# Sliding-window attention into an RWKV channel mix: how the first q and k are loaded, which batches are transposed by the crossbar, and how the planner is set

## The chip, the cores and the metric

One core of a Trainium2 chip runs the whole kernel. The metric is the device time of one execution in microseconds (us). The kernel before takes 235.64 us (median of 14 runs, 234.65 to 236.24). The engines are TensorE (PE, matmul and transpose), ScalarE (ACT), VectorE (DVE), GpSimd (POOL, which here issues nearly all the loads), SyncE (SP, which issues stores and crossbar transposes) and 16 DMA engines.

## What is computed

q, k and v have 8 batches, 8 heads, 576 positions and a head dimension of 64, in fp32. Cut to what matters:

```python
scores = scale * q @ k.T                      # per batch and head
scores = where(0 <= i - j < 128, scores - slope[h] * abs(i - j), -1e9)
attn   = softmax(scores) @ v                  # causal window of 128
x      = attn, heads side by side             # [8, 576, 512]
x_prev = x shifted by one position
xk = mu_k * x + (1 - mu_k) * x_prev           # xr the same with mu_r
k  = relu(xk @ w_k)                           # 512 -> 1024
out = sigmoid(xr @ w_r) * ((k * k) @ w_v)     # 1024 -> 512
```

## The kernel before

**Stages.** Each of the eight batches is cut into four pairs of heads (g = 0 to 3). A pair goes through these steps: q and k are brought into a layout with the head dimension on the partitions; PE multiplies k by q (`scores`, L658), with the ALiBi bias added by a matmul (L645) in batch 0 and by a multiplication with a mask on DVE (L685) in the later batches; ACT takes the exponential (L672); PE multiplies by v (`attend`, L716), with a column of ones for the sum; DVE takes the reciprocal and scales (L722, L727); PE transposes the result (`out_t` L754 or `out_some` L771) and ACT copies it into `xt` (L628); DVE makes the difference and the two mixes `xk` and `xr` (`shift`, L814 and L821). `channel_mix` then does, for a stretch of 256, 384 or 512 positions, eight products with w_k (L907), each with a relu on ACT (L914) and a square on DVE (L880), and then for each 128 positions a product with w_r (L925, tanh on ACT, L932) and one with w_v in two halves (L941), joined on DVE (L946) and stored.

**How q and k come into that layout.** There are five ways. In batch 0 the work is done in two parts, positions 0 to 255 and the rest. In part 0 the first two pairs (g = 0, 1) are loaded as fp32 in runs of two positions (512 bytes), cast to bf16 by DVE (`CAST`) and transposed as bf16 (L1049); pairs 2 and 3, listed in `FT`, are loaded row by row (256 bytes) and transposed as fp32 by PE (L1046). Part 1 of batch 0 and the batches in `WIDE` are loaded with a cast on the way in long runs (`run_load`, L434) and transposed in 64 x 64 quarters (`qk_quad`, L1002), with two copies out of PSUM. Other batches are loaded row by row (`full_load`, L463) and transposed 128 x 128 (`qk_full`, L1154), with one copy. Batches in `XB` are loaded row by row and transposed by the DMA crossbar (`flip`). The last 64 positions (the tail) of q and k are loaded by `tail_load` (L453) and transposed on PE (L856), or by the crossbar for the batches in `XTT`.

**Order.** A planner simulates the kernel with its own costs and writes out each engine's instruction order; the engines then run in that order and wait on semaphores. Attention and channel mix compete by a rank: attention pair number 4b + g gets the key (4b + g - A) x SLOPE, with an A for each engine, and a piece of channel mix gets the sum of PE time of the channel mix ahead of it. A larger A puts attention further ahead. On PE, work in 64-row mode may be put off by `WAIT` so that it meets other work of that mode. Ninety matmuls of a dummy tile (L619, `warm`) have the lowest rank and fill PE where it has nothing else, early in the run.

**Loads.** POOL issues loads in one fixed order, after the first q (on SP's queue) and k (on ACT's queue). The string `LOADS` gives it for the first part: v and V are the halves of v of batch 0; 2 and 3 are part 1 of q and k, for heads 0 to 3 and 4 to 7; K and k are the halves of w_k; t is the tail of batch 0; a, b and c are q and k, tail, and v of batch 1; R is w_r; W and w are the halves of w_v. Batches 2 to 7 follow, each as a, b, c.

```python
    LOADS = 'v23KtVkabcRWw'
    A = {PE: 14.25, ACT: 4.00, DVE: 4.50, VIR: 0}
    WIDE = (1,)
    FT = (2, 3)
```

Of the kernel before, what the change touches and what calls it, by code (L numbers as in the profile page):

```python
# [179 lines left out]
def kernel(  # L180
# [12 lines left out]
    nc = tc.nc  # L193

    B, H, S, D = q.shape
    DM = H * D
    DF = moe_w_k.shape[1]
    G = H // 2
    NF = S // 128
# [7 lines left out]
    SM = 128 * NF  # L207
    RELU_SCALE = 0.5 ** 0.5

    PE, ACT, DVE, POOL, SPE, FAB, VIR = "PE", "ACT", "DVE", "POOL", "SP", "FAB", "VIR"  # L210
    NQ, NA, NX, NV, NC = 4, 4, 3, 2, 2
    XB = range(5, B)
    XO = range(6, B)
    X0 = 16
    NWARM = 90
    LOADS = 'v23KtVkabcRWw'
    XD = 6
    OTL = 1.5
    FIN = 384
    RATE = 284.0  # L220
    WIDE = (1,)
    PART_WIDE = True
    QUAD = 0.0565
    RUN = {2: 64 * 284 / 329.0, NF: 128 * 284 / 357.0}
    FLIP = 1.25
    NO = 5
    WAIT = 2.0
    QM = 0
    OM = 1

    def XU(b, g):
        return (DVE,)

    def SQ(order):
        return (DVE,)

    XT0 = (ACT,)
    QK0 = (ACT, DVE)
    CAST = (DVE,)
    FT = (2, 3)  # L240
    KQ = ACT
    VCUT = True
    XTT = range(6, B)
    MMASK = False
    VDEP = 1
    TCOST = 1.5
# [14 lines left out]
    ts_buf = many(2, [128, H, D], BF16, "ts")  # L261
    tt_buf = many(2, [128, G, 3, 64], BF16, "tt")
# [23 lines left out]
    ident = cst.tile([128, 128], BF16, name="ident")  # L286
# [16 lines left out]
    def one(h):  # L303
        return uno[h.idx if h.cls == "p1" else N1 + h.idx]

    def two(h):
        return duo[h.idx]

    plan = Plan(dict(qx=2, xb=2, p2=2, p1=N1, pt=4 - N1, qk=NQ, at=NA, xu=NX, vs=NV, cb=NC, ts=2, tt=2, xt=2, dl=2, dl0=4,
                     xk=2, rl=3, kk=3, rs=4, ot=NO),  # L310
                {}, WAIT)
# [5 lines left out]
    def act_t(n, sb=False):  # L317
        return (n + (112 if sb else 61)) / 1200.0

    def dve_t(n, fast=1):  # L320
        return (n / fast + 66) / 960.0

    AHEAD = 30.0
    A = {PE: 14.25, ACT: 4.00, DVE: 4.50, VIR: 0}
    NBIAS = 4
    XRL = 3.0
    MODE = 0
    EARLY = 0.0
    SLOPE = 4.5

    def rank(prio):

# [9 lines left out]
    def op(e, dur, deps, prio, emit, need=(), free=()):  # L342
        prio = rank(prio)
        return plan.add(e, dur, LAT.get(e, 0.2) if isinstance(e, str) else LAT[e[0]] if len(e) == 1 else 0.22,
                        deps, prio, emit, need, free)

    last = {}

    def virtual(key, holds):
        n = plan.add(VIR, 0.0001, 0.0001, [last.get(key)], (0,), None, holds)  # L350
        last[key] = n
        return n
# [11 lines left out]
    def dma(queue, kb, issue, emit, deps=(), need=(), free=(), lat=(1.0, 0.9)):  # L364
        n = plan.add(queue, issue, 0.0, list(deps) + [last.get(queue)],
                     (len(plan.nodes),), emit, need)
        last[queue] = n
        return fab(queue, kb / RATE, n, lat, free)
# [38 lines left out]
    n_ident = dve_op(0.11, emit_ident, [n_iota], (0, -1))  # L407
# [21 lines left out]
    def issue_t(nd):  # L429
        return 0.53 + 0.00034 * nd  # L430
# [16 lines left out]
    def tail_load(b):  # L447
        h = Hold("ts")
        g = virtual("ts", [h])
        ns = []  # L450
        for i in range(2):
            src = (q, k)[i][b, :, SM:S].rearrange("h p d -> p h d")
            ns.append(dma(POOL, 128 * TCOST, issue_t(512), lambda e, i=i, src=src: nc.gpsimd.dma_start(  # L453
                out=ts_buf[h.idx][64 * i:64 * i + 64], in_=src), [g]))
        return h, ns
# [4 lines left out]
    def full_load(b, i, h, g):  # L460
        src = (q, k)[i][b, :, 0:SM].rearrange(
            "h (r p) d -> p h r d" if b in XB else "h (p r) d -> p h r d", p=128)
        return [dma(POOL, 256, issue_t(1024), lambda e, r=r: nc.gpsimd.dma_start(  # L463
# [58 lines left out]
    th, tl, n_w, src1 = {}, {}, {}, {}  # L522
# [31 lines left out]
    cw, ch, cl, xbh, xbl, tth, ttl, ttg = {}, {}, {}, {}, {}, {}, {}, {}  # L554
# [10 lines left out]
    def batch_load(b, what):  # L565
# [7 lines left out]
        elif what == "b":  # L573
            th[b], tl[b] = tail_load(b)
            if b in XB:
                xbh[b] = Hold("qx")
# [20 lines left out]
    for (c0, n) in DSEG:  # L597
        n_copy[c0] = dve_op(dve_t(n, 4), lambda e, c0=c0, n=n: nc.vector.tensor_copy(
            out=dist[:, c0:c0 + n], in_=dist[:, 0:n]), [n_dist], (0, 1))
    n_sid = [dve_op(0.1, lambda e, h=h: nc.vector.tensor_scalar(  # L600
        out=sid[:, h], in0=ident, scalar1=-(2.0 ** (-(h + 1))) / scale, scalar2=None,
# [6 lines left out]
    def emit_mu(e):  # L608
# [5 lines left out]
        out=mu_sb.rearrange("p i o -> p (i o)"), in_=one(h_mu)[:, 0:2 * NPO]), (), [h_mu])  # L614
# [12 lines left out]
    def copy_any(e, out, in_):  # L627
        (nc.scalar.copy if e == ACT else nc.vector.tensor_copy)(out=out, in_=in_)  # L628
# [213 lines left out]
            res.append(fab(SPE, 1.0 * rows / 128, n, (1.0, 0.9), [hx]))  # L842
        return res

    def tails(b, prio):
        htt = Hold("tt")
        hs = th[b]
        if b in XTT:
            plan.follow(last["tt"], ttg[b])
            last["tt"] = ttg[b]  # L850
            return tth[b], ttl[b]
        hp = Hold("p1")

        def emit(e):
            for g in range(G):
                nc.tensor.transpose(  # L856
                    one(hp).bitcast(BF16)[:, 128 * g:128 * g + 128],
                    ts_buf[hs.idx][:, 2 * g:2 * g + 2].rearrange("p h d -> p (h d)"), ident)

        def emit_c(e):  # L860
            copy_any(e, tt_buf[htt.idx][:, :, 0:2].rearrange("p g t c -> p g (t c)"),
                     one(hp).bitcast(BF16)[:, 0:128 * G].rearrange("p (g w) -> p g w", g=G))

        t = op(PE, 0.0565 * G, list(tl[b]) + [n_ident], prio + (0,), emit, [hp], [hs])
        g = virtual("tt", [htt])
        c = [op(DVE, dve_t(512), [t, g], prio + (0,), emit_c, (), [hp])]
        return htt, c


# [2 lines left out]

    n_hw = 39 + sum(4 if g in FT else 2 for g in range(3)) + 8 * len(XB) + len(XTT) + NJ * len(XO)
    n_split = -n_hw % 8
# [119 lines left out]
    def qk_quad(b, g, nr, buf, deps, prio, c0, hq, take, free):  # L994

        hp = [Hold("p1"), Hold("p1")]

        def emit(e):
            for n in range(2 * nr):
                for hl, r in ((0, 0), (1, 1), (1, 0), (0, 1)):  # L1000
                    rows = slice(64 * r, 64 * r + 64)
                    nc.tensor.transpose(  # L1002
                        one(hp[r]).bitcast(BF16)[64 * hl:64 * hl + 64, 64 * n:64 * n + 64],
                        buf()[rows, n // nr, 2 * g + hl, n % nr], ident[rows, rows])

        t = op(PE, QUAD * 2 * nr, list(deps) + [n_ident], prio + (3,), emit,
               hp + ([hq] if take else []), free)
        t.rows, t.lazy = (64, 64), True
        w = 64 * nr
        ys = [op(QK0 if b == 0 else ACT, {ACT: act_t(2 * w), DVE: dve_t(2 * w)}, [t], prio + (3,),  # L1010
                 lambda e, r=r: copy_any(
            e, qk_buf[hq.idx][:, :, c0 + w * r:c0 + w * r + w].rearrange("p t (c r) -> p t c r", r=nr),
            one(hp[r]).bitcast(BF16)[:, 0:2 * w].rearrange("p (t r c) -> p t c r", t=2, r=nr)),
                 (), [hp[r]]) for r in range(2)]
        return hq, ys
# [6 lines left out]
    for part in range(2):  # L1022
        if part == 1:
            htt, n_tt = tails(0, (0, 0, 1, 0))
        for g in range(G):
            prio = (0, 0, part, g)
# [12 lines left out]
            hp = Hold("p1") if part == 0 else None  # L1039
# [13 lines left out]
            if part:  # L1053
                ys = qk_quad(0, g, 2, lambda: part_buf, cs, prio, 256, hq0[g], False, [])[1]
            else:
                cold = 1.8 if part == 0 and g < 2 else 1.0
                t = op(PE, (0.115 if f32 else 0.0565) * 4 * cold, cs + [n_ident], prio + (3,), emit_t,
                       [hp] + ([hq0[g]] if part == 0 else []))
                ys = [op(QK0, {ACT: act_t(512), DVE: dve_t(512)}, [t], prio + (3,),
                       lambda e, part=part, g=g, hp=hp, f32=f32: copy_any(  # L1060
                    e, qk_buf[hq0[g].idx][:, :, 0:256],
                    one(hp).rearrange("p (t c) -> p t c", t=2)) if f32 else copy_any(
                    e, qk_buf[hq0[g].idx][:, :, 256 * part:256 * part + 256].rearrange(
                        "p t (c r) -> p t c r", r=2),
                    one(hp).bitcast(BF16)[:, 0:512].rearrange("p (t r c) -> p t c r", t=2, r=2)),
                    (), [hp])]
            ha = Hold("at")
            es = []
            for j, (pieces, m0) in enumerate(PART[part]):
# [8 lines left out]
            r, hx = attend(0, g, t0, t1, ha, es + vl[0][0:2] + (vl[0][2:] + blank if part else []),  # L1078
                           prio)
            a, c = out_t(0, g, t0, t1, hx, [r], prio, xh[0], xth[0], late if part == 0 else None)  # L1080
# [31 lines left out]
    for j, (c0, n) in enumerate(MSEG):  # L1112
        n_mcopy.append(op(DVE, dve_t(8 * n, 4), ms + n_mcopy, (2, j),
                          lambda e, c0=c0, n=n: nc.vector.tensor_copy(
            out=mask[:, 0:H, c0:c0 + n], in_=mask[:, 0:H, 0:n])))
# [48 lines left out]
    for b in range(1, B):  # L1164
# [6 lines left out]
        htt, n_tt = tails(b, (0, b, 0, 0))  # L1171
        for g in range(G):
            prio = (0, b, 0, g)
            ha = Hold("at")
            if b in XB:
                hq, y = xbh[b], xbl[b]
# [13 lines left out]
            r, hx = attend(b, g, 0, NJ, ha, [m0, m1] + vl[b] + rs[0:1], prio)  # L1190
# [60 lines left out]
```

The softmax here doesn't subtract the row's maximum and nothing guards it: scores larger than these inputs give would overflow.

## Time and profile before

| | us |
|---|---|
| median of 14 runs | 235.64 (234.65 to 236.24) |
| the profiled execution | 235.28 |
| its span, first to last instruction | 233.2 |
| PE busy | 225.6 |
| DVE busy | 189.2 |
| ACT busy | 160.7 |
| POOL busy | 97.7 |

Busy time is what an engine's instructions cover in the span. A PE instruction is shown with its latency, so that two neighbours overlap, and what one costs is the distance from its start to the next one's; gaps shorter than that latency, and the dummy matmuls, count as busy. In a row of the order of time, the first number is the start, the second the length of the group, and "xN" how many instructions it holds. The granted clock is 0.999.

### The profile page before, as it was taken

Reading aid. Unit: us, or ns where it says so; the run is one execution under the profiler, and the core shown is the slowest. Engines: PE = TensorE matmul, PEld = TensorE weight load, DVE = VectorE, ACT = ScalarE, POOL = GpSimd, SP = SyncE. Lnnn points to the kernel's source line nnn. Section 1 sums busy time; section 2 is a strip of 40 time slices with the busy share of each in tenths; the row PEclk is TensorE's granted clock in tenths of the full one; section 3 lists DMA queues with packets and bytes.
Section 4 is the critical chain, followed back from the end, with each engine's and each line's share of the span. In section 5 each row is a group of like instructions: output and inputs, shape, how many; then the busy total and the mean of one; then the engine's idle time right before and its main releaser. Section 6 shows DMA issues by size and latency. Waiting matters only on the chain.

```text
span 233.2 us, 6268 instructions
## 1 busy us (share of the span) xinstructions
PE 225.6 (97%) x2487; PEld 135.7 (58%) x2487; DVE 189.2 (81%) x427; ACT 160.7 (69%) x292; POOL 97.7 (42%) x124
## 2 busy tenths in 40 slices
PE   8899989999999999999999999999999999999994
PEld 6466765456565765555555755454655844455462
DVE  7577978987897989989989979985869996974242
ACT  3569999759998986984984975947594726326251
POOL 8967683898882893068608845200000000000000
PEclk9999999999999999999999999999999999999999
DMA  7999999999999999779999999993242124121122
GB/s 167 178 170 196 163 173 182 155 201 199 155 138 174 105 143 203 112 93 175 205 150 135 172 176 170 172 155 122 70 92 93 45 48 146 46 90 48 64 71 90
DMA packets 131100, 31.73 MB, mean 136 GB/s; under 512 B 120056, under 2 KB 127232, under 8 KB 131072
## 3 DMA queue, kind: packets, MB, share of 16 engines
q0 software_dynamic: 102736, 16.26, 101.6%
q1 hardware_dynamic: 26592, 14.50, 27.1%
q10 hardware_dynamic: 1744, 0.59, 1.0%
q8 instruction: 19, 0.31, 0.6%
q14 instruction: 9, 0.07, 0.1%
HBM read 33.56 MB, written 9.44 MB: 184 GB/s over the span
## 4 chain that ended last, share of the span: by engine, by line
PE 87%; ACT 5%; DMA 2%; DVE 2%; issue 2%; SPq 1%; DVEq 0%; ACTq 0%
PE uno L941 27%; PE uno L907 26%; PE uno L925 14%; PE duo L716 6%; PE duo L658 6%; DMA qx<-in_q_dram 2%; PE uno L771 2%; PE uno L1154 2%; ACT at L672 2%; ACT mask L1088 1%; ACT qk L628 1%; PE uno L856 1%; ACT xt L628 1%; ACT rl L914 1%; PE uno L619 1%
## 5 line engine op out<-in xcount | busy, mean ns | idle before, releaser
L941 PE MATMUL uno<-wv_sb,kk 128*128 128x512 bf16 (+2 forms) x296 | 71.8, 374 | 0.0
L907 PE MATMUL uno<-xk,wk_sb 128*128 128x256 bf16 (+2 forms) x416 | 69.5, 314 | 0.6 <-ACT rl L914 0.4
L672 ACT ACTIVATE at<-duo 128x1024 bf16<-128x1024 f32 (+2 forms) x68 | 65.8, 1005 | 5.4 <-PE duo L658 5.4
L914 ACT ACTIVATE rl<-uno 128x256 bf16<-128x256 f32 (+2 forms) x104 | 47.4, 494 | 20.2 <-PE uno L907 19.0
L907 PEld LDWEIGHTS <-wk_sb 128*128 128x128 bf16 x416 | 38.7, 98 | 22.1 <-issue 0.9
L685 DVE TENSOR_TENSOR at<-at,mask 128x1024 bf16<-128x1024 bf16 x56 | 37.8, 681 | 8.1 <-ACT at L672 7.8
L438 POOL DMA_DIRECT2D vs<-in_v_dram x32 | 28.3, 898 | 34.1 <-PE duo L716 31.5
L941 PEld LDWEIGHTS <-kk 128*128 128x128 bf16 x296 | 26.4, 98 | 26.2
L880 DVE TENSOR_TENSOR kk<-rl 128x256 bf16<-128x256 bf16 (+2 forms) x104 | 33.1, 336 | 9.3 <-ACT rl L914 8.0
L932 ACT ACTIVATE rs<-uno 128x512 bf16<-128x512 f32 x36 | 22.2, 616 | 26.1 <-PE uno L925 23.1
L925 PE MATMUL uno<-wr_sb,xr 128*128 128x512 bf16 x144 | 37.0, 379 | 0.5 <-ACT rl L914 0.5
L946 DVE SCALAR_TENSOR_TENSOR ot<-rs,uno 128x512 f32<-128x512 bf16 (+2 forms) x37 | 24.7, 669 | 12.1 <-PE uno L941 9.7
L716 PEld LDWEIGHTS <-at 128*128 128x128 bf16 x576 | 21.8, 98 | 6.0 <-issue 0.9
L821 DVE SCALAR_TENSOR_TENSOR xk<-dl,mu_sb,xt 128x576 bf16<-128x576 bf16 (+1 forms) x32 | 24.8, 781 | 0.4
L821 DVE SCALAR_TENSOR_TENSOR xr<-dl,mu_sb,xt 128x576 bf16<-128x576 bf16 (+1 forms) x32 | 24.5, 771 | 0.0
L463 POOL DMA_DIRECT2D cb<-in_k_dram x24 | 21.3, 908 | 7.2 <-DMA wv_sb<-in_moe_w_v_dram 3.3
L628 ACT COPY xt<-uno 128x256 bf16<-128x256 bf16 (+1 forms) x48 | 17.1, 406 | 9.0 <-PE uno L771 8.8
L925 PEld LDWEIGHTS <-xr 128*128 128x128 bf16 x144 | 13.5, 98 | 14.6 <-issue 0.7
L463 POOL DMA_DIRECT2D cb<-in_q_dram x24 | 21.3, 921 | 1.2 <-DMA vs<-in_v_dram 1.0
L628 ACT COPY qk<-uno 128x1024 bf16<-128x1024 bf16 (+2 forms) x26 | 18.9, 779 | 2.5 <-PE uno L1002 1.1
L716 PE MATMUL duo<-vs,at 128*128 128x65 bf16 x448 | 19.1, 193 | 0.0
L814 DVE TENSOR_TENSOR dl<-xt 128x576 bf16<-128x576 bf16 (+1 forms) x32 | 13.8, 435 | 4.2 <-ACT xt L628 4.2
(78 smaller groups left out, 206.1 us busy)
## 6 DMA issues: line engine op xcount, KB each, us to landing
out_dram<-ot SPq DMA_DIRECT2D x30, 256.0 KB, 5.1
vs<-in_v_dram POOLq DMA_DIRECT2D x32, 128.0 KB, 7.0
cb<-in_q_dram POOLq DMA_DIRECT2D x24, 128.0 KB, 7.2
cb<-in_k_dram POOLq DMA_DIRECT2D x24, 128.0 KB, 7.2
out_dram<-ot SPq DMA_DIRECT2D x10, 128.0 KB, 1.8
wk_sb<-in_moe_w_k_dram POOLq DMA_DIRECT2D x2, 512.0 KB, 8.9
wv_sb<-in_moe_w_v_dram POOLq DMA_DIRECT2D x2, 512.0 KB, 10.2
qx<-in_k_dram ACTq DMA_DIRECT2D x4, 128.0 KB, 4.6
```

Source lines behind the costliest of these rows:

```text
L438: return dma(POOL, 256, issue_t(1024), lambda e: nc.gpsimd.dma_start(out=vs_buf[h.idx][:, j, :, 0:D], in_=v[b, :, 128 * j:128 * j + 128].r ...
L463: return [dma(POOL, 256, issue_t(1024), lambda e, r=r: nc.gpsimd.dma_start(out=cb_buf[h.idx][:, i, r], in_=src[:, :, r]), [g]) for r in ra ...
L628: (nc.scalar.copy if e == ACT else nc.vector.tensor_copy)(out=out, in_=in_)
L672: lambda e, ah=ah, w=w, hp=hp: nc.scalar.activation(out=ah(), in_=two(hp)[:, :, 0:w], func=AF.Exp, scale=float(scale)), (), [hp])
L685: nc.vector.tensor_tensor(out=a, in0=a, in1=m, op=ALU.mult)
L716: nc.tensor.matmul(a[:, hl, t - t0], lhsT=at[:, lo:lo + 128], rhs=vs[:, u, 2 * g + hl, :] if u < NF else tvb[:, 2 * g + hl], start=(u == u ...
L821: lambda e: nc.vector.scalar_tensor_tensor(out=buf[hk.idx][:, g, e0 + c0:e0 + c1], in0=dls(), scalar=mu[:, g:g + 1], in1=xc(1), op0=ALU.mu ...
L880: nc.vector.tensor_tensor(out=out, in0=in_, in1=in_, op=ALU.mult)
L907: nc.tensor.matmul(one(hp)[:, 0:n], lhsT=wk_sb[:, po, 128 * fo:128 * fo + 128], rhs=xk_buf[hx.idx][:, po, c0:c1], start=(po == 0), stop=(p ...
L914: a = op(ACT, act_t(n), [s], pr, lambda e, hp=hp, hr=hr: nc.scalar.activation(out=rl_buf[hr.idx][:, 0:n], in_=one(hp)[:, 0:n], func=AF.Rel ...
L925: nc.tensor.matmul(one(hp), lhsT=xr_buf[hx.idx][:, po, 128 * c:128 * c + 128], rhs=wr_sb[:, po], start=(po == 0), stop=(po == NPO - 1))
L941: nc.tensor.matmul(one(hv)[:, a:b], lhsT=kk_buf[hk.idx][:, fo, o:o + 128], rhs=wv_sb[:, fo, a:b], start=(fo == 0), stop=(fo == NFO - 1))
```

## The change

All four pairs of batch 0's part 0 are loaded in 512-byte runs and cast by DVE (`FT` is empty). Batch 2 joins batch 1 in the long-run load and the quarter transposes. Batches 3 and 4 go from `qk_full` to `qk_some` (two pairs in one go, 64-row transposes, `QM` = 2), and so does batch 5, which leaves the crossbar. The result of attention goes from `out_some` to `out_t` (128-row transposes, one copy, `OM` = 0). Tails of batches 4 and 5 go to the crossbar. The tail of batch 0 is loaded in runs of four positions and transposed by 16 small matmuls. Copies of q and k of batches 1 and 2 may go to DVE as well as ACT, and squares of the first three stretches to ACT as well as DVE. The first half of w_k is loaded ahead of part 1 of q and k, and w_r ahead of v of batch 1. The planner's leads, slope, waits and costs change.

```diff
-    XB = range(5, B)
+    XB = range(6, B)
...
-    LOADS = 'v23KtVkabcRWw'
-    XD = 6
+    LOADS = 'vK23tVkabRcWw'
+    XD = 4
...
-    WIDE = (1,)
+    WIDE = (1, 2)
...
-    QUAD = 0.0565
-    RUN = {2: 64 * 284 / 329.0, NF: 128 * 284 / 357.0}
+    QK1 = (ACT, DVE)
+    TW = (0,)
+    QUAD = 0.040
+    RUN = {2: 64 * 284 / 345.0, NF: 128 * 284 / 390.0}
...
-    WAIT = 2.0
-    QM = 0
-    OM = 1
+    WAIT = 1.0
+    QM = 2
+    OM = 0
...
-        return (DVE,)
+        return (DVE, ACT) if order < 3 else (DVE,)
...
-    FT = (2, 3)
+    FT = ()
...
-    XTT = range(6, B)
+    XTT = range(4, B)
...
-    A = {PE: 14.25, ACT: 4.00, DVE: 4.50, VIR: 0}
+    A = {PE: 7.75, ACT: 4.50, DVE: 4.00, VIR: 0}
...
-    XRL = 3.0
+    XRL = 4.0
...
-    SLOPE = 4.5
+    SLOPE = 4.7
...
+        if b in TW:
+            for i in range(2):
+                ns.append(dma(POOL, 104, issue_t(128), lambda e, i=i: nc.gpsimd.dma_start(
+                    out=ts_buf[h.idx].rearrange("p h d -> p (h d)")[:, 256 * i:256 * i + 256],
+                    in_=(q, k)[i][b, :, SM:S].rearrange("h (c r) d -> h c (r d)", r=4)), [g]))
+            return h, ns
...
+    def tails_full(b, prio, htt, hs):
...
+        if b not in TW:
+            return tails_full(b, prio, htt, hs)
         hp = Hold("p1")
         def emit(e):
+            for n in range(8):
+                for hl in range(2):
+                    nc.tensor.matmul(
+                        one(hp)[64 * hl:64 * hl + 64, 64 * n:64 * n + 64],
+                        lhsT=ts_buf[hs.idx][:, n],
+                        rhs=ident.rearrange("p (g t c) -> p t g c", g=G, t=2)[:, hl],
+                        start=True, stop=True)
...
+        c = [op(DVE, dve_t(256), [t, g], prio + (0,), lambda e, i=i: copy_any(
+            e, tt_buf[htt.idx][:, :, i].rearrange("p g (c r) -> p g c r", r=4),
+            one(hp)[:, 256 * i:256 * i + 256].rearrange("p (r g c) -> p g c r", r=4, g=G)),
+                (), [hp]) for i in range(2)]
...
-        ys = [op(QK0 if b == 0 else ACT, {ACT: act_t(2 * w), DVE: dve_t(2 * w)}, [t], prio + (3,),
+        ys = [op(QK0 if b == 0 else QK1, {ACT: act_t(2 * w), DVE: dve_t(2 * w)}, [t], prio + (3,),
```

More of the change, by code (lines that the diff above doesn't have):

```diff
@@ L843, in out_flip @@
         return res
[L845 to L851, printed above, removed]
+    def tails_full(b, prio, htt, hs):
         hp = Hold("p1")
@@ L866, in tails, with emit @@
         c = [op(DVE, dve_t(512), [t, g], prio + (0,), emit_c, (), [hp])]
+        return htt, c
+    def tails(b, prio):
+        htt = Hold("tt")
+        hs = th[b]
+        if b in XTT:
+            plan.follow(last["tt"], ttg[b])
+            last["tt"] = ttg[b]
+            return tth[b], ttl[b]
+        if b not in TW:
+            return tails_full(b, prio, htt, hs)
+        hp = Hold("p1")
+        def emit(e):
+            for n in range(8):
[5 more added lines that the diff above has]
+                        start=True, stop=True)
+        t = op(PE, 0.03 * 16, list(tl[b]) + [n_ident], prio + (0,), emit, [hp], [hs])
+        g = virtual("tt", [htt])
+        c = [op(DVE, dve_t(256), [t, g], prio + (0,), lambda e, i=i: copy_any(
+            e, tt_buf[htt.idx][:, :, i].rearrange("p g (c r) -> p g c r", r=4),
+            one(hp)[:, 256 * i:256 * i + 256].rearrange("p (r g c) -> p g c r", r=4, g=G)),
+                (), [hp]) for i in range(2)]
         return htt, c
```

## The prediction

> **What bounds the kernel now.** I read the page's busy totals first, then busy time by stage, then the longest waits, then the order of time in the first 40 us.
>
> ```profile
> PE 225.6 (97%) x2487; PEld 135.7 (58%) x2487; DVE 189.2 (81%) x427; ACT 160.7 (69%) x292; POOL 97.7 (42%) x124
> 20.00:30.00 10.00, 9.38 (x222) 7.44 (x221) 8.65 (x28) 9.71 (x28) 7.09 (x10) 1.00 2.03 168
> 30.00:40.00 10.00, 9.05 (x146) 6.56 (x146) 7.64 (x21) 9.67 (x20) 5.89 (x7) 1.00 1.55 187
> 40.00:230.00 190.00, 189.72 (x1868) 109.48 (x1866) 157.87 (x317) 129.60 (x226) 69.32 (x83) 1.00 1.25 127
> ```
>
> The columns of the last three lines are PE, its weight loads, DVE, ACT, POOL. From 40 us to 230 us PE is busy for 189.72 of 190 us: whatever PE work is added or removed there moves the end one for one, and nothing else does. From 20 to 40 us ACT is the full engine (9.71 and 9.67 of 10), with DVE at 8.65 and 7.64. Ahead of 20 us (PE 7.81 and 9.65) PE's busy time is partly the dummy matmuls. So there are two sums: PE work, and how soon the first 40 us get real work into PE.
>
> ```profile
> 7.78 1.07 PE L1046 MATMUL uno<-id,qx 128*128 128x128 f32 x7 [0.85 <-DMA qx<-in_q_dram]
> 8.68 0.39 PE L619 MATMUL uno<-warm 128*128 128x128 bf16 x4
> 9.26 0.61 PE L716 MATMUL uno<-vs,at 128*128 128x65 bf16 x12 [0.20 <-DVE qk L628]
> 13.52 0.84 PE L619 MATMUL uno<-warm 128*128 128x128 bf16 x12
> 15.95 0.83 PE L619 MATMUL uno<-warm 128*128 128x128 bf16 x12
> 18.96 0.61 PE L907 MATMUL uno<-xk,wk_sb 128*128 128x256 bf16 x4
> ```
>
> The fp32 pairs arrive at 7.7 us, and PE waits for them. Of the 90 dummies 57 come after 8.6 us; at 56 ns each that is 3.2 us of filler. The first channel mix starts at 18.96 us. By distances between starts, PE spends some 10 us between 4 and 40 us on filler and waits.
>
> [...]
>
> ```profile
> 50.00 1.04 PE L941 MATMUL uno<-wv_sb,kk 128*128 128x512 bf16 x4
> 50.97 0.32 PE L771 MATMUL uno<-ident,xu 64*128 64x64 bf16 x10
> 51.22 0.62 PE L1154 MATMUL uno<-ident,cb 128*128 128x128 bf16 x8
> 51.68 1.03 PE L941 MATMUL uno<-wv_sb,kk 128*128 128x512 bf16 x4
> 52.54 0.39 PE L856 MATMUL uno<-ident,ts 128*128 128x128 bf16 x4
> 52.76 1.50 PE L1154 MATMUL uno<-ident,cb 128*128 128x128 bf16 x24
> ```
>
> Four L941 take 0.86 us between neighbours of the same mode (51.68 to 52.54) but 0.97 before the 64-row L771: 0.10 into the mode, about 0.12 out of it. [...] in the DMA view of 2 to 8 us the queues move 283 to 340 GB/s while the 512-byte runs of pairs 0 and 1 arrive, and 184 to 276 when the 256-byte rows follow. [...]
>
> **The change, part by part: PE after 40 us.**
> - Results of attention, batches 1 to 5, 20 pairs. Ten 64-row transposes take 0.15 us beside scores (which are in that mode anyway), and about 0.14 + 0.22 = 0.36 alone. In the order of time 12 stand beside scores and 8 alone: 12 x 0.16 + 8 x 0.36 = 4.8 us. The five 128-row transposes at 56 ns (eight L1154 take 0.46) are 0.28: 5.6 us. **+0.8.**
> - q and k of batches 3 and 4. Before: 8 x 0.45 = 3.6 us. After: four groups of 32 64-row transposes. The row of L771 gives 14.4 ns each, so 0.46, and 0.02 to 0.22 of mode change: 1.9 to 2.7. **-1.3.**
> - Batch 5 leaves the crossbar: two such groups. **+1.15** (0.96 to 1.35).
> - Batch 2 in quarters: 32 quarter transposes take 0.34 to 0.40 us by the L1002 rows, plus mode change 0.02 to 0.22, against 0.45. Four pairs: -0.4 to +0.7. **0** taken.
> - Tails of batches 4 and 5: two L856 groups at 0.22 (52.54 to 52.76). **-0.45.**
>
> The sum is +0.2 us; ends -1.2 and +1.8. ACT, DVE and SP carry the rest under PE after 40 us: one copy of 576 columns in place of 428 + 383 ns, two copies of 620 ns in place of one of 1045 per pair, eight crossbar transposes fewer and two more. ACT has 60 us free there, DVE 32. If that cover went, DVE would be the first to be late.
>
> **The first 40 us.**
> - Load of pairs 2 and 3. 2048 packets of 256 B become 1024 of 512 B. At 230 and 320 GB/s the 0.52 MB take 2.3 and 1.6 us: **0.7 earlier**, so 7.0 us. Then two DVE casts per pair (0.42 each) replace none: g = 2 is cast at 7.9, transposed by 8.2 and copied by 8.9, where before its two products started at 10.13 (behind the attend at 9.26 that waited on DVE's 0.69 us fp32 copy). I take **0.8 us** earlier for both pairs. DVE's memsets end at 7.15 in the kernel before, so the casts find it free; were they late, the gain would be 0. PE's eight fp32 transposes (138 ns apart) become eight of 56: 0.6 us in a stretch with slack.
> - w_k ahead of part 1. The POOL issue moves it past four loads (0.76 us each), and they move past it: one issue (0.78) and 512 KB of bf16 at the 175 GB/s of that stretch, 2.9 us. Part 1's first quarter transposes were at 11.10, so the data that came by about 10.7 now comes at 13 to 13.6 (0.7 is given back by the shorter first loads). The four groups of that transpose were at 11.10, 13.27, 15.58 and 17.46, so three of four have room; what is queued behind the first on PE is attend and the output transposes of part 0, which go ahead in the new order. In exchange channel mix can start as soon as xk of part 0 is there. I cost the exchange at 0, with -1 to +2 us as its ends.
> - Tail of batch 0: 1024 packets of 128 B become 256 of 512 B; at 150 and 195 GB/s that is 0.87 against 0.67 us. Sixteen matmuls in place of four transposes and two DVE copies in place of one stand where the dummies stood: 0.
> - q and k of batch 1 come about 0.9 us earlier (0.7 + 0.2). Their first transpose waited until 25.47.
> - w_r ahead of v of batch 1: w_r lands some 6 us earlier, and L925 (first at 37.57) can fill PE. v is pushed back by 512 KB at 197 GB/s, 2.7 us: from 33.3 to 35.1 with the 0.9 above. The first attend of batch 1 was at 36.37, which leaves 1.2 us. w_v does not move by order, only by the 0.9: L941 could not start before it in either kernel.
> - ACT in 20 to 40 us: eight copies of q and k at 0.62 us (5.0 us); if DVE takes half, ACT is freed of 2.5 us and DVE pays 4 x 0.69 = 2.8 of its 3.7 free. One copy for two in `out_t` gives 4 x 0.16. ACT's stage shortens by up to 3 us; what is late next is DVE, then v and w_v. I take half: **1.5 us**.
>
> Sum: -0.8 - 1.5 + 0.2 = **-2.1 us**. From the profiled execution's 235.28 (span 233.2, 2.1 around it) that is 233.2, and against the median, 0.36 higher, **233.5 us**. Runs of this kernel scatter by 0.3%, so I call within 0.2% (0.5 us) the same.
>
> **The rivals.**
> 1. *The shorter lead makes it slower.* On PE attention's lead falls from A = 14.25 to 7.75. The channel mix is 62 + 31 + 62 = 156 us of PE, 4.9 per pair, 19.5 per batch. The last pair of batch b ranks at 18b - 51 before and 18.8b - 22 after, against its own mix at 19.5b: some 51 us of cover become 22. A pair's path from scores to xk is some 8 to 10 us in the trace when nothing stands in front, and ACT's and DVE's own leads are short. DVE is at 9.8 of 10 in some stretches (40 to 50, 90 to 100 us). If a batch boundary catches PE without mix work, each of the six boundaries costs about 1 us: minus 2 becomes plus 4, 239; with half of them, 237. For it: the cover is more than halved. Against: 22 us is still twice the path. It decides once queueing adds more than 12 us to the path.
> 2. *The early gain is hidden.* PE cannot have its w_v work before w_v lands (about 38 us) and v of batch 1 comes later; what ACT and DVE save is waited away. Then only the PE sum (+0.2) and 0.3 to 0.8 of start remain: 235.6 + 0.2 - 0.5 = 235.3. This includes that the casts don't bring pairs 2 and 3 forward.
> 3. *The start gains more.* The exchange of w_k gives its whole 1 us, ACT's stage its 3 us, and grouping with scores brings the PE sum to -0.2: 235.6 - 0.8 - 1 - 3 - 0.2 = 230.6.
>
> **How the numbers follow.** Forecast (232 to 235.1): 0.47. Rival 3: 0.10. Rival 2: 0.14. Rival 1, with its milder forms: 0.29. Faster by over 0.2%: 0.57; within: 0.13; slower: 0.30. The range reaches down to rival 3's end and up through the milder half of rival 1: 230.6 to 238.0. The forecast's own range is 232 to 235.1.
>
> **What would show it.** Right: first scores of pairs 2 and 3 near 9 us instead of 10.1; channel mix starting near 16 to 17 us instead of 18.96 and fewer dummies after 8 us; ACT below 9.5 of 10 in 20 to 40 us, with q and k copies on DVE; PE still over 99% busy from 40 us. Wrong: PE idle in the middle, ended by DVE's xk, xr or squares (rival 1); PE's start of full occupation still at 40 us (rival 2); or more mode changes than I counted for the 64-row groups.

## The result, and the profile after

The changed kernel takes 237.93 us (median of 10 runs, 237.28 to 238.38) against 235.50 for the kernel before beside it (48 runs). The ratio is 1.01, with a 95% interval of 1.0083 to 1.0118: slower by 1%, where I had forecast 0.9% faster. The profiled execution has a span of 235.8 us against 233.2.

The page's busy totals, and busy time by stage (PE, its weight loads, DVE, ACT, POOL), of the kernel after:

```profile
PE 225.8 (96%) x2615; PEld 138.0 (59%) x2615; DVE 190.4 (81%) x420; ACT 166.3 (71%) x302; POOL 93.6 (40%) x120
20.00:30.00 10.00, 9.69 (x211) 7.54 (x210) 8.12 (x24) 10.00 (x30) 6.21 (x9) 1.00 1.62 188
30.00:40.00 10.00, 9.90 (x170) 7.30 (x160) 9.17 (x18) 10.00 (x23) 5.85 (x8) 1.00 1.76 182
40.00:230.00 190.00, 186.65 (x1964) 109.55 (x1964) 156.04 (x311) 133.98 (x230) 66.19 (x79) 1.00 1.19 123
```

From 20 to 40 us PE idles only 0.4 us, where it idled 1.6 before. ACT, which I expected to be relieved, is at 10.00 of 10. And from 40 to 230 us, where PE was busy for 189.72, it is busy for 186.65: 3.1 us of new idle time. The first 20 us, of the kernel before (two rows) and of the kernel after (two rows):

```profile
0.00:10.00 10.00, 7.81 (x79) 5.87 (x79) 6.63 (x39) 4.55 (x6) 8.49 (x17) 1.00 1.23 169
10.00:20.00 10.00, 9.65 (x180) 6.33 (x179) 7.99 (x25) 7.14 (x16) 6.92 (x10) 1.00 1.80 180
0.00:10.00 10.00, 7.75 (x87) 5.63 (x88) 7.45 (x42) 4.86 (x7) 8.68 (x17) 1.00 1.06 172
10.00:20.00 10.00, 9.22 (x188) 6.43 (x185) 8.16 (x26) 6.87 (x16) 6.65 (x10) 1.00 1.83 172
```

These rows say where the time went. Up to 40 us PE is busy for 35.9 us before and for 36.6 us after, with the same 90 dummies in both and none of them later: the start gained 0.7 us. PE's busy total grew by 0.2 us (225.6 to 225.8). After 40 us PE idles 3.1 us more. 0.2 - 0.7 + 3.1 is 2.6 us, the difference of the two spans. So the whole loss stands after 40 us. The waits of PE there in the kernel after, in us in total, times, longest (the kernel before has one, of 0.2):

```profile
PE uno L937 <- DVE xk L829: 1.8, 1, 1.8
PE duo L724 <- ACT at L680: 0.7, 1, 0.7
PE uno L955 <- ACT qk L636: 0.6, 1, 0.6
PE uno L937 <- ACT rl L944: 0.2, 1, 0.2
```

The first three are the w_k product of the last batch (211 us), an attend (78 us) and a w_r product (67 us). ACT's order of time around the w_r product shows three copies of q and k in a row behind two exponentials; PE waits for one of these copies:

```profile
63.41 1.96 ACT L680 ACTIVATE at<-duo 128x1024 bf16<-128x1024 f32 x2
65.23 1.60 ACT L636 COPY qk<-uno 128x512 bf16<-128x512 bf16 x3
66.65 2.03 ACT L680 ACTIVATE at<-duo 128x1024 bf16<-128x1024 f32 x2
```

The wait at 211 us is for DVE. DVE's order puts joins of the channel mix (`ot`) between the pieces of the last batch's shift, and DVE sits idle for 2.46 us ahead of the first of them:

```profile
202.11 0.69 DVE L976 SCALAR_TENSOR_TENSOR ot<-rs,uno 128x512 f32<-128x512 bf16 x1 [2.46 <-PE uno L971]
209.77 0.68 DVE L976 SCALAR_TENSOR_TENSOR ot<-rs,uno 128x512 f32<-128x512 bf16 x1
210.37 0.81 DVE L829 SCALAR_TENSOR_TENSOR xk<-dl,mu_sb,xt 128x576 bf16<-128x576 bf16 x1
```

SP, too, issues its last five crossbar transposes into `xt` later, from 193.95 us on and not from 189.04.

What ACT had taken on, by the groups of ACT in the kernel after with their shapes:

```profile
L636 ACT COPY qk<-uno 128x512 bf16<-128x512 bf16 x37 | 21.6, 631 | 3.4 <-PE uno L1079 2.5 <-PE uno L1032 0.9
L908 ACT ACTIVATE kk<-rl 128x256 bf16<-128x256 bf16 x12 | 5.1, 487 | 0.0
L908 ACT ACTIVATE kk<-rl 128x384 bf16<-128x384 bf16 x3 | 1.5, 563 | 0.0
```

L908 is the square, which was on DVE alone. Fifteen of them, 6.6 us, now stand on ACT. A square of 256 columns takes 487 ns there; on DVE it took 283 in the kernel before. Of the sixteen 512-column copies of q and k of batches 1 and 2 only six went to DVE.

### The profile page after: what moved, and what is told of

Its sections match the earlier page's. It is cut to its first block, busy times and chain, and to the rows that moved or that the text cites. A ratio compares the mean times of both kernels' runs of the same rounds, so it can differ in the third digit from the quotient of the medians.

```text
span 235.8 us, 6507 instructions
## 1 busy us (share of the span) xinstructions
PE 225.8 (96%) x2615; PEld 138.0 (59%) x2615; DVE 190.4 (81%) x420; ACT 166.3 (71%) x302; POOL 93.6 (40%) x120
## 4 chain that ended last, share of the span: by engine, by line
PE 82%; ACT 5%; DVE 4%; DMA 4%; POOL 3%; issue 1%; DVEq 0%; POOLq 0%; ACTq 0%
PE uno L971 25%; PE uno L937 25%; PE uno L955 13%; PE duo L724 6%; PE duo L666 6%; DMA ts<-in_k_dram 4%; PE uno L762 2%; POOL qx L436 1%; ACT qk L636 1%; ACT rl L944 1%; DVE ot L976 1%; PE duo L653 1%; DVE xk L829 1%; ACT at L680 1%; POOL vs L440 1%
## 5 line engine op out<-in xcount | busy, mean ns | idle before, releaser
L680 ACT ACTIVATE at<-duo 128x1024 bf16<-128x1024 f32 (+2 forms) x68 | 64.4, 996 | 7.4 <-PE duo L666 7.3
L944 ACT ACTIVATE rl<-uno 128x256 bf16<-128x256 f32 (+2 forms) x104 | 47.9, 493 | 22.5 <-PE uno L937 20.8
L693 DVE TENSOR_TENSOR at<-at,mask 128x1024 bf16<-128x1024 bf16 x56 | 36.8, 680 | 1.8 <-ACT at L680 1.6
L910 DVE TENSOR_TENSOR kk<-rl 128x256 bf16<-128x256 bf16 (+2 forms) x89 | 29.5, 343 | 9.6 <-ACT rl L944 8.4
L636 ACT COPY qk<-uno 128x512 bf16<-128x512 bf16 (+1 forms) x42 | 23.3, 600 | 4.8 <-PE uno L1079 2.5
L636 ACT COPY xt<-uno 128x576 bf16<-128x576 bf16 (+2 forms) x28 | 16.2, 586 | 5.3 <-PE uno L762 5.3
L471 POOL DMA_DIRECT2D cb<-in_k_dram x20 | 17.8, 913 | 2.4 <-DMA vs<-in_v_dram 1.3
L471 POOL DMA_DIRECT2D cb<-in_q_dram x20 | 17.7, 917 | 2.1 <-PE uno L955 0.9
L735 DVE TENSOR_TENSOR xu<-duo,rc 128x640 bf16<-128x640 f32 x20 | 16.4, 820 | 0.4
```

The costliest lines, as they stand in the source:

```text
L680: lambda e, ah=ah, w=w, hp=hp: nc.scalar.activation(out=ah(), in_=two(hp)[:, :, 0:w], func=AF.Exp, scale=float(scale)), (), [hp])
L693: nc.vector.tensor_tensor(out=a, in0=a, in1=m, op=ALU.mult)
L910: nc.vector.tensor_tensor(out=out, in0=in_, in1=in_, op=ALU.mult)
L944: a = op(ACT, act_t(n), [s], pr, lambda e, hp=hp, hr=hr: nc.scalar.activation(out=rl_buf[hr.idx][:, 0:n], in_=one(hp)[:, 0:n], func=AF.Rel ...
```

## The experiments

Two theories first. **Theory 1** is rival 1 of the prediction: attention's shorter lead lets PE run out of channel mix. **Theory 2**: the work itself, batch 5 above all. Later ones come as the runs raise them.

**The leads.** `a_oldleads`: the kernel after with the old planner settings. `b_newleads`: the kernel before with the new ones. `a_xb5`: batch 5 back on the crossbar.

```diff
-    A = {PE: 7.75, ACT: 4.50, DVE: 4.00, VIR: 0}
+    A = {PE: 14.25, ACT: 4.00, DVE: 4.50, VIR: 0}
...
-    SLOPE = 4.7
+    SLOPE = 4.5
```

> The kernel after with the planner's five settings of the kernel before (A, SLOPE, XRL, XD, WAIT); loads, casts, transposes and batches as in the change. Theory 1 (the shorter lead makes PE run out of channel mix): PE's idle time after 40 us falls from 3.3 us to under 0.6 us and the time to 234 to 235 us. Theory 2 (the work itself, with batch 5 on PE and ACT and 128-row output transposes, is what costs): idle time stays over 2 us or PE work grows, and the time stays at 237 to 239 us.

> The kernel before with the five planner settings of the change and nothing else. Theory 1: PE idles 2 to 4 us after 40 us, 237.5 to 239.5 us. Theory 2: within 1 us of the kernel before, 234.7 to 236.5 us.

```diff
-    XB = range(6, B)
+    XB = range(5, B)
```

> The kernel after with batch 5 given back to the crossbar. Theory 2: PE loses about 1.1 us of transposes and ACT 5 us of copies, so the stalls of the middle and of the last batch shrink: 235 to 236.5 us. Theory 1: PE loses its 1.1 us at most and the last batch's stall of 1.8 us stays: 236.5 to 238 us.

Measured, in this order: 238.75 us (ratio to before 1.0148, 1.0104 to 1.0191); 235.98 (1.0011, 0.9986 to 1.0037); 236.39 (1.0036, 1.0023 to 1.0048). Theory 1 falls from both sides: the old leads don't help the new kernel, and the new leads don't measurably hurt the old one. The last batch's wait of 1.8 us is gone with the old leads, but others take its place (the longest 1.2 and 0.6 us). Giving batch 5 back gains 1.5 us, which lies just inside theory 2's range; but the stalls at 67 and 78 us, which theory 2 expected to shrink, stay, and so does a wait of 1.2 us for the last batch.

**The start, the squares, the transposes.** `b_ft_loads` makes two of the early edits alone in the kernel before:

```diff
-    LOADS = 'v23KtVkabcRWw'
+    LOADS = 'vK23tVkabRcWw'
...
-    FT = (2, 3)
+    FT = ()
```

> The kernel before with the two early edits alone: all four first pairs in 512-byte runs with casts on DVE, and the new order of loads (w_k ahead of part 1, w_r ahead of v of batch 1). By my prediction's steps pairs 2 and 3 gain 0.8 us and the order of loads nothing: 234.2 to 235.2 us. If the start is what costs, 236.5 us or more.

Measured: 236.43 us (1.0045, 1.0027 to 1.0063), 1.0 slower. Then single parts were put back in the kernel after: `QM` from 2 to 0 (`a_qm0`), `OM` from 0 to 1 (`a_om1`), `SQ` to DVE alone (`a_sqdve`), and `FT`, `LOADS` and `TW` to what they were (`a_oldstart`).

> The kernel after with batches 3, 4 and 5 back to one pair at a time (128-row transposes, one PSUM tile, one copy of 1045 ns). Theory 3 (the grouped transposes take two of four single PSUM tiles and put two or four copies of 620 ns in a row on ACT, and PE waits for both): the stalls of 0.59 and 0.73 us near 66 and 77 us go, PE gets some 2 to 2.7 us more transposes, and the time is 237 to 239 us, near the kernel after. Theory 4 (the time is PE's work alone, with stalls as chance): slower than the kernel after by 2 us, 239.5 to 241 us.

> The kernel after with output transposes in 64-row form again. By my prediction's step these are worth 0.8 us of PE: 236.5 to 237.5 us. By the difference of the two traces (PE spends 5.0 us on them before and 7.9 after) they would be worth up to 2.9 us: 235 to 236 us.

> The kernel after with all squares on DVE. Theory 5 (squares put on ACT keep it full from 20 to 40 us, 10.00 of 10, and eat the relief that the copies on DVE gave): ACT falls below 9.7 of 10 there and the time falls by 0.5 to 1.5 us, to 236.5 to 237.5 us. If DVE is the one that sets that stretch, the time rises by 0.5 us or more.

> The kernel after with the start of the kernel before: fp32 transposes for pairs 2 and 3, the old order of loads, the tail of batch 0 row by row. From the run of the kernel before with the new start (1.0 us slower): 236.5 to 237.3 us. By my prediction's steps (the new start gains 0.8 us): 238.3 to 239 us.

| run | us | ratio to before (95%) |
|---|---|---|
| a_qm0 | 237.35 | 1.0076 (1.0049 to 1.0102) |
| a_om1 | 237.64 | 1.0086 (1.0060 to 1.0113) |
| a_sqdve | 236.19 | 1.0046 (1.0026 to 1.0066) |
| a_oldstart | 236.73 | 1.0045 (1.0028 to 1.0063) |

Every one is faster than the kernel after, by 0.6, 0.3, 1.7 and 1.2 us (`a_om1` lies outside both of its ranges). In `a_qm0` PE waits for nothing after 40 us any more, so theory 3's stalls are real, but PE is busy for 2.0 us more (227.8), which takes most of the 3.1 us back. The squares are worth most, more than theory 5 said. In `a_sqdve`, by stage:

```profile
20.00:30.00 10.00, 9.13 (x215) 7.28 (x213) 8.68 (x26) 8.88 (x25) 6.18 (x9) 1.00 1.63 186
30.00:40.00 10.00, 9.75 (x166) 6.84 (x153) 9.70 (x24) 9.14 (x17) 5.23 (x7) 1.00 1.76 181
40.00:230.00 190.00, 188.23 (x1972) 110.94 (x1971) 158.78 (x319) 130.80 (x224) 66.19 (x79) 1.00 1.23 122
```

ACT comes down to 8.88 and 9.14, which is the relief that I had forecast for the change, and PE's idle time from 40 to 230 us falls from 3.3 to 1.8 us; the wait for the last batch's xk is gone.

**Do the parts add up?**

> The kernel before with the one edit that lets the planner put squares of the first three stretches on ACT. Theory 5 (squares on ACT fill it from 20 to 60 us): ACT busier by 3 us or more from 20 to 60 us and 0.5 to 2 us slower, 236.0 to 237.5 us. If ACT's squares are free relief for DVE: 234.5 to 235.5 us.

> The kernel before with all four first pairs in 512-byte runs and casts on DVE, the order of loads unchanged. If the new order of loads is what made the new start slower (1.0 us): 234.5 to 235.4 us, the gain of up to 0.8 us that I forecast. If the casts are: 236 to 236.8 us.

> The kernel after with the start of the kernel before and all squares on DVE. If the two costs add up (1.2 and 1.7 us): 235.0 us, level with the kernel before. If they are one cost seen twice: 236.0 to 236.7 us.

> As the run before it, and batch 5 given back to the crossbar. If that cost adds up too (1.5 us): 233.5 to 234.3 us, faster than both kernels. If the three remove the same stalls: 235 to 236.5 us.

Measured: `b_sq`, squares also on ACT in the kernel before, 237.23 us (1.0068, 1.0047 to 1.0089), as theory 5 says. `b_ft`, the casts alone, 240.57 (1.0212, 1.0172 to 1.0252): twice the slowdown of the whole change, for an edit of the first 8 us. `c_old_sq` 236.21 (1.0031, 1.0003 to 1.0059) and `c_old_sq_xb5` 236.93 (1.0065, 1.0046 to 1.0084): the gains of the single edits don't add, and giving batch 5 back, worth 1.5 us alone, here costs 0.7. `c_old_sq` still has a wait of 1.7 us for the last batch's xk. `b_ft` shows where most of its time went: PE's 3.0 us of waits after 40 us (0.2 in the kernel before) all come between 53 and 72 us, long after the edit. These are the three longest, in us in total, times, longest:

```profile
PE duo L658 <- ACT at L672: 1.1, 1, 1.1
PE uno L907 <- ACT rl L914: 0.6, 1, 0.6
PE uno L907 <- DVE xk L821: 0.6, 1, 0.6
```

Hence **theory 6**: every edit makes the planner write a new order of the whole kernel, and that order can move the time by as much as the edit.

**The order held.** In three runs the order of every engine was kept as in the kernel before and one part alone was edited. `b_ft_pin` swaps the loads, casts and transposes of pairs 2 and 3, with the planner still counting the fp32 form. `b_loads_pin` moves two loads in the finished order. `b_sq_pin` gives every second square of the first three stretches to ACT at its place:

```diff
-        for n in plan.run():
+        for n in first(first(plan.run(), n_w['k', 0].base, src1[0][0].base), n_w['r'].base, vl[1][0].base):
...
-                e, kk_buf[hk.idx][:, fo, 0:n], rl_buf[hr.idx][:, 0:n]), (), [hr]))
+                ACT if order < 3 and fo % 2 else e, kk_buf[hk.idx][:, fo, 0:n], rl_buf[hr.idx][:, 0:n]), (), [hr]))
```

`b_rate` is the counterpart: the planner's DMA rate goes from 284 to 282, the same instructions in a new order.

> The kernel before with all four first pairs in 512-byte runs, cast by DVE and transposed as bf16, but with every engine's order held as it was (only these loads, casts and transposes differ). Theory 6 (an edit moves the time mostly by making the planner write a new order of the whole kernel): 234.6 to 235.7 us, where the same edit with a new plan took 240.6. Theory 7 (the casts themselves cost): 238 us or more.

> The kernel before with the loads of the first half of w_k and of w_r moved ahead as in the change, all engines' orders otherwise held. Part 1 of q and k comes later under an order made for the old arrival: by my prediction -1 to +2 us, 234.6 to 237.6 us. Theory 6 alone would have it within 0.7 us of the kernel before; more than 1 us slower shows that the order of loads costs by itself.

> The kernel before with 12 of the 24 squares of the first three stretches on ACT, each at its place in the held order. Theory 5 (ACT is the full engine there): slower by 0.7 to 2.5 us, 236.2 to 238 us. Theory 6 alone: within 0.7 us of the kernel before.

> The kernel before with only the planner's figure for the DMA rate changed from 284 to 282: the same instructions in another order. Theory 6: the time moves by 0.5 us or more either way, rather up since the old order was the chosen one, 236 to 238 us. Without theory 6: within 0.5 us, 235.0 to 236.0 us.

| run | us | ratio to before (95%) | difference from 235.50 |
|---|---|---|---|
| b_ft_pin | 235.51 | 0.9988 (0.9971 to 1.0005) | 0.0 |
| b_loads_pin | 237.87 | 1.0096 (1.0074 to 1.0118) | +2.4 |
| b_sq_pin | 237.52 | 1.0088 (1.0079 to 1.0097) | +2.0 |
| b_rate | 236.42 | 1.0034 (1.0015 to 1.0052) | +0.9 |

The casts cost nothing that can be measured, so the 5.1 us of `b_ft` were the order. A new order without any edit of the instructions costs 0.9 us (`b_newleads`, which is another such order, 0.5, within the noise). Under the held order loads and squares cost 2 us or more each by themselves. In `b_sq_pin`, by stage, ACT fills up and PE is busy for 1.2 us less than in the kernel before (17.20 against 18.43 of 20):

```profile
20.00:30.00 10.00, 9.23 (x217) 7.41 (x218) 8.28 (x24) 9.97 (x30) 6.76 (x9) 1.00 2.04 168
30.00:40.00 10.00, 7.96 (x126) 5.88 (x127) 6.07 (x14) 9.79 (x22) 5.78 (x7) 1.00 1.58 188
```

As the order is the same, starts can be compared too: the transposes of batch 1 start at 25.13 us, 0.3 earlier than in the kernel before, and the first product with w_r at 38.76, 1.2 later. So 1.5 of the 2.0 us are lost between these two. DVE's busy time falls by 1.9 us in the two stages, about what the squares that left them had taken (2.1).

In `b_loads_pin`, PE's order of time shows part 1 waiting for its data, with the channel mix and everything else queued behind it:

```profile
10.98 0.34 PE L658 MATMUL duo<-qk 64*128 64x256 bf16 x4
12.53 0.25 PE L1002 MATMUL uno<-ident,qx 64*64 64x64 bf16 x8 [1.21 <-DMA qx<-in_q_dram]
13.30 0.26 PE L1002 MATMUL uno<-ident,qx 64*64 64x64 bf16 x8 [0.51 <-DMA qx<-in_k_dram]
13.69 0.71 PE L619 MATMUL uno<-warm 128*128 128x128 bf16 x5
```

**Both taken out of the change.** `a_loads` gives the kernel after the old `LOADS`; `a_loads_sq` also keeps the squares on DVE.

> The kernel after with the old order of loads alone (casts, tail of batch 0 and all else as in the change). With the order held, the new order of loads cost the kernel before 2.3 us. If it costs the kernel after as much: 235.2 to 236.2 us. If the kernel after, planned for this order, pays little: 237 to 238.3 us.

> The kernel after with the old order of loads and all squares on DVE: the two edits that cost with the order held, taken out; the casts, the long runs, the grouped transposes, the batches and the planner settings of the change stay. If these two are the cause: 234.5 to 235.8 us, level with the kernel before or better. If the rest of the change costs by itself: 236.2 us or more.

Measured: 237.66 us (1.0102, 1.0075 to 1.0129) and 235.63 (1.0009, 0.9996 to 1.0022). The old order of loads alone gives the kernel after 0.3 us, which is within the noise: the kernel after, planned for the new order of loads, puts part 1 later and fills the place with dummies. The two together give back the whole slowdown, and the squares are the larger part of it: 2.0 us between these two runs, 1.7 between the kernel after and `a_sqdve`. Five pairs of runs differ in the squares, one with the order held and four with an order planned anew: squares on ACT are slower by 2.0 us in the first, by 1.7, 1.8 and 2.0 in three others, and by 0.5, within the noise, in the last (`c_old_sq` against `a_oldstart`). No version was measurably faster than the kernel before.

What stays open: apart from the three held ones, each of these kernels has its own planned order, and a new order alone moved the time by 0.9 us, in `b_ft` by 5.1. So the differences of 0.3 to 0.6 us (`a_loads`, `a_om1`, `a_qm0`) can't be told from the order. That batch 5, the grouped transposes and the wide batch 2 together cost about nothing rests on `a_loads_sq` alone. And how squares on ACT make the kernel after slower is not shown. They fill ACT from 20 to 40 us, but PE is not short of work there, and the last of them is over at 62 us, ahead of all three long waits. `a_qm0` has ACT as full in these 20 us and no such wait; `c_old_sq` has no square on ACT and the wait of 1.7 us. So part of the 1.7 to 2.0 us may be the orders that the planner wrote with and without them.

## Why the prediction was wrong, step by step

- **The cover after 40 us (put at 0).** This step failed, and the traces have the whole loss here. The prediction said that after 40 us PE work moves the end "and nothing else does", since ACT has 60 us free there and DVE 32. PE work came as forecast (busy +0.2 us), but PE waited for 3.1 us more: 1.8 for DVE's xk, 0.7 for an exponential and 0.6 for a copy, both on ACT. Free time summed over 190 us doesn't say whether one result is there when PE's order comes to it. The prediction named DVE as the first to be late, and the longest wait is DVE's.
- **ACT in 20 to 40 us (forecast -1.5 us).** This step failed as well. It counted the copies that leave ACT and not the squares that come with the change's line on `SQ`. In these 20 us five 512-column copies left ACT (3.1 us at 0.62) and eleven squares came (4.7 us); in all there are fifteen, 6.6 us. ACT went from 19.38 us of 20 to 20.00. All steps of the first 40 us together brought 0.7 us of PE work, where I had put 2.3. With the squares off ACT the step's size is right (ACT 1.4 us less busy in these 20 us than in the kernel before), but the time only comes back to near level.
- **Pairs 2 and 3 (forecast 0.8 us earlier).** Right in place and size for the first: its products start at 9.31 us, not 10.13; those of pair 3 at 10.38, not 10.84. Wrong in worth: the first channel mix starts at 19.49 us, where it had been 18.96 and I had said 16 to 17, and with the order held the edit is worth 0.0 us. Getting a pair ready sooner did not shorten what follows.
- **w_k ahead of part 1 (forecast 0, ends -1 and +2).** The data came when I said (first quarter transposes at 13.29, forecast 13 to 13.6). The value depends on the order: +2.4 us with the order held, past the end of +2, and 0.3 at most in the kernel after. The argument for 0, that three of four groups have room, looked at the groups and not at the PE queue, where under the held order all later work stands behind the first of them. In the kernel after the tail of batch 0 also came late, and PE waited for it, which I had put at 0:

```profile
16.99 0.32 PE L885 MATMUL uno<-ident,ts 128*64 128x64 bf16 x8 [0.54 <-DMA ts<-in_k_dram]
```

- **w_r ahead of v of batch 1.** Right: the first product with w_r starts at 31.50 us, not 37.57, and the first attend of batch 1 at 35.62, not 36.37.
- **PE work (forecast +0.2 us, -1.2 to +1.8).** The sum was right: PE's busy total grew by 0.2 us. By distances from start to start, waits left out, output transposes went from 5.0 to 7.9 us (I said 4.8 to 5.6 for the later batches, plus 1.1 of batch 0 in both), q and k of the later batches from 7.3 to 6.9, the 128-row tails from 1.6 to 0.8 with 0.6 new for batch 0. A 64-row group cost 0.57 us, inside the ends I gave. The output transposes cost more by this count than I said, and the products with w_k, w_r and w_v 1.2 us less; a change of mode counts in the row ahead of it (a 512-column product with w_v takes 0.31 us from its start to the next one's ahead of 64-row work, and 0.22 elsewhere), and there are 92 changes, not 102. What the output transposes are worth on their own is not shown: the run with 64-row outputs again gained only 0.3 us.
- **Rival 1.** Its symptom came (PE idle in the middle and at the last batch, 3.1 us); its cause didn't: `a_qm0`, `a_oldstart` and `a_sqdve` have the same leads and 0.2, 1.0 and 1.8 us of idle time from 40 to 230 us. That the time came out between rival 1's two prices is luck. (By its own numbers these are 239.5 and 236.5 us, not 239 and 237.)

## What to carry to other kernels

Where an engine is full in a stage, go through every line of a change that lets work onto it, permission to a planner included. Here the planner's formula gave a square of 256 columns 0.31 us on ACT and 0.20 on DVE; the traces show 0.49 and 0.28, so it underrated both, and ACT by more. The trace of the kernel before has prices near it, a relu of 256 columns at 418 ns on ACT (L914) and an exponential of 256 bf16 columns at 446 ns (L1088), so a price well above 0.31 us could have been had ahead of the run. And don't take free time summed over a long stage for cover: look at when each result is ready and when it is asked for. Where a planner writes the order, an edit and its new order are two changes: hold the order to price the edit, and make a new order without an edit to see how far the order alone moves the time.

## What the runs showed of the hardware

In two traces the granted clock fell after a stretch in which PE had little work. In `b_loads_pin` PE is busy for 2.3 of the 4 us from 10 to 14 us, with marked waits of 1.21 and 0.51 us and little work between them; the granted clock is 0.86 from 12 to 14 us, 0.50 from 14 to 16 and 0.79 from 16 to 18. By stage, with the granted clock third from the end:

```profile
12.00:14.00 2.00, 0.96 (x21) 0.78 (x22) 0.40 (x2) 0.23 (x1) 1.85 (x3) 0.86 1.93 173
14.00:16.00 2.00, 2.00 (x20) 1.53 (x18) 1.10 (x6) 0.75 (x2) 1.94 (x3) 0.50 2.41 158
16.00:18.00 2.00, 2.00 (x43) 1.50 (x43) 1.11 (x5) 1.30 (x3) 1.27 (x2) 0.79 2.21 153
```

Eleven of its 20 executions have a mean clock under 0.996, with a median of 238.5 us; the other nine have 236.8. My estimate from these medians: of its +2.4 us some 1.3 are the wait for the loads, and the rest goes with the clock. Of the 63 runs of the kernel before beside it, one has such a clock. The trace of `b_ft_pin` shows the same: PE is busy for 1.8 of the 4 us from 6 to 10 us, and the granted clock is 0.66 from 10 to 12 us, 0.50 from 12 to 14 and 0.99 from 14 to 16; two of its 20 executions have a mean clock under 0.996. In `b_newleads`, on the other hand, PE is busy for 2.3 of the 4 us from 6 to 10 us and the clock stays at 1.00 up to 22 us, and in the kernel after it is 1.00 through the wait of 1.8 us at 211 us, from 209 to 215 us. No run here varies a gap alone, so what brings the clock down, and how much idle time it takes, is not shown. The dummy matmuls, which I had counted as mere filler, stand where such gaps would be; no run takes them away, so what they are worth is not shown either.
